# Hashed attention and channel mix on one core: bucket rows on GpSimd, joined bits in the first pair, and a new order

## The chip, the core and the metric

The kernel runs on one core of a Trainium2 chip. The metric is the device time of one execution in microseconds (us); the time of a kernel is the median of its runs. A profile is one execution, taken by the hardware profiler. TensorE multiplies matrices (PE in the profile, PEld its weight loads), VectorE (DVE) and GpSimd (POOL) do elementwise work, ScalarE (ACT) does functions such as the exponential, and SyncE (SP) issues transfers (DMAs). Each engine takes its instructions in the order in which the program gives them.

## What is computed

Attention in which a query sees only keys of its own hash bucket (six sign bits of a projection), for 4 batches of 8 heads, 768 positions, 64 channels; then a channel mix over the 512 channels of each batch.

```python
q_bits = (np.einsum('bhsd,dk->bhsk', q, proj) > 0)
k_bits = (np.einsum('bhsd,dk->bhsk', k, proj) > 0)
mask = q_bucket[:, :, :, None] == k_bucket[:, :, None, :]
scores = np.where(mask, scale * np.matmul(q, k.transpose(0, 1, 3, 2)), -1e9)
attn = softmax(scores); x = heads joined(np.matmul(attn, v))
xk = mu_k * x + (1.0 - mu_k) * x_prev      # x_prev: x one position earlier
xr = mu_r * x + (1.0 - mu_r) * x_prev
kk = np.maximum(xk @ w_k, 0.0)
out = sigmoid(xr @ w_r) * (kk * kk @ w_v)
```

## The kernel before

The work goes by pairs of heads, 16 of them, four to a batch. For a pair, q and k of its two heads are loaded (`nat`), scaled and split into a high and a low half-precision part (`nh`: `hi`, line 495 or 555; `lo`, line 498 or 560), and transposed into `a`, 128 rows deep with positions along the free axis: from pair 2 on by one transposing DMA (line 502), for pairs 0 and 1 by TensorE (line 573) with a copy out of PSUM (lines 578 and 580).

The bucket mask is part of the score matmul: six rows of `a`, 64 to 69, hold the sign bits of q (scaled) and of k, so that equal buckets add a constant that the exponential's bias takes off again. To get these rows, TensorE multiplies `a` by the projection (`bits`, line 521), VectorE turns the signs into numbers in `bx` (line 524), 32 partitions to each of the four blocks q0, q1, k0, k1, and four DMAs on SyncE's queue move six partitions each from `bx` to rows 64 to 69 of `a` (`row`, line 534). For pair 0 alone each block has its own matmul (line 597) and its own sign operation, which writes the rows of `a` at once (line 605 on VectorE, 603 on ScalarE); `DIRECT = (0,)` says so.

Scores come in nine steps of 1024 columns a pair (`sc`, line 637), each followed by one exponential on ScalarE into `pt` (line 641). Then the product with v (`oo`, line 666), the normalization (lines 677 to 684), a transpose of the result, by TensorE (`ot`, line 694) or by DMA (`otd`, line 700), the mix with the previous position (`df`, `xk`, `xr`, lines 725 to 740). GpSimd sums v (lines 446 to 458) and casts the weights (line 405). Once the four pairs of a batch are there, the channel mix runs: `kp` (line 758) with a relu (762) and a square (765), `r` (779) with a tanh (782), `v` (789), the last product (796) and the store (799) for each of six chunks of 128 positions.

Every operation is recorded by `add` with the engine it runs on, and issued in the order of the list `ORDER`, a permutation of all operations written out in the file. So the order on each engine is that of `ORDER`, and a waiting operation holds all that stand behind it on its engine. PSUM has eight banks; `schedule` gives a bank, or a pair of them, to each result that asks for one with `take`, as a plan with estimated durations finds them free.

Of the kernel before, what the change touches and what calls it, by code (L numbers as in the profile page):

```python
# [12 lines left out]
U16 = mybir.dt.uint16  # L13
# [4 lines left out]
LAG = {"PE": 0.21, "ACT": 0.21, "DVE": 0.15, "POOL": 0.18, "SP": 1.8, "GQ": 2.0}  # L18

PR = {  # L20
    'ldq': -2.811, 'ldv': -2.337, 'hi': -5.393, 'lo': -1.084, 'tr': -2.122, 'bits': -1.224, 'bx': -4.393, 'row': 4.034,
    'va': 0.273, 'vsum': -2.003, 'mean': -0.515, 'pv0': 0.767, 'pv1': 1.128, 'fin': -1.916, 'ot': 1.215, 'xt': -1.326,
    'df': -1.607, 'xk': -3.487, 'xr': 2.133, 'moe': 4.97, 'mk': 2.095, 'mv': 2.279, 'sq': 0.189, 'os': 0.275,
    'tpe': -4.352, 'tev': -0.289, 'va_u': 2.059, 'vsum_u': -3.477,
    'otd': 1.3, 'wk': 1.5, 'wkd': 0.2, 'wr': 3.0, 'wrd': 0.1, 'wv': 3.4, 'wvd': 0.1, 'wc': 0.5, 'p0b': -8.0, 'p0j': 0.6, 'p0n': 8.0,
}


PX = {}


def X(kind, n):
    return PX.get(f"{kind}@{n}", 0.0)


def R(kind, n):
    return n + PR[kind] + X(kind, n)


ORDER = [  # L40
    16, 17, 23, 21, 14, 20, 55, 56, 19, 25, 0, 2, 3, 4, 63, 64, 83, 5, 84, 6, 7, 8, 10, 69,
    58, 89, 70, 13, 57, 73, 65, 66, 26, 27, 85, 28, 29, 30, 67, 90, 91, 92, 86, 87, 68, 74, 75, 76,
    79, 80, 93, 94, 61, 71, 106, 114, 107, 108, 60, 115, 22, 18, 102, 31, 81, 88, 82, 110, 109, 77, 95, 165,
    159, 116, 11, 96, 12, 59, 136, 137, 72, 132, 133, 103, 104, 111, 112, 166, 105, 15, 212, 158, 211, 113, 62, 134,
    167, 138, 78, 117, 135, 168, 118, 119, 264, 121, 139, 126, 127, 123, 169, 170, 218, 130, 131, 120, 122, 219, 140, 98,
    99, 100, 101, 147, 124, 148, 220, 221, 222, 223, 128, 141, 149, 150, 125, 142, 35, 129, 143, 191, 192, 151, 193, 144,
    145, 146, 194, 189, 271, 190, 171, 172, 177, 181, 178, 182, 174, 179, 180, 161, 187, 188, 272, 152, 153, 154, 185, 186,
    162, 32, 163, 164, 195, 183, 184, 155, 156, 224, 225, 176, 246, 247, 200, 242, 243, 240, 241, 201, 265, 424, 425, 244,
    97, 245, 196, 197, 198, 175, 173, 232, 233, 202, 214, 215, 234, 235, 199, 230, 231, 238, 273, 36, 203, 239, 204, 205,
    206, 207, 229, 274, 275, 208, 33, 34, 210, 227, 292, 160, 296, 157, 216, 217, 253, 293, 290, 226, 209, 248, 236, 228,  # L50
    297, 288, 291, 254, 294, 249, 267, 268, 269, 237, 289, 426, 255, 256, 286, 250, 251, 295, 284, 252, 257, 213, 287, 427,
    280, 285, 270, 417, 303, 282, 414, 415, 428, 281, 277, 479, 480, 283, 278, 418, 276, 435, 419, 436, 279, 449, 450, 304,
    305, 298, 445, 306, 299, 300, 446, 307, 301, 37, 441, 442, 443, 444, 420, 302, 41, 308, 421, 38, 422, 423, 42, 39,
    447, 432, 437, 448, 438, 309, 430, 258, 504, 505, 456, 500, 501, 259, 310, 260, 261, 43, 457, 458, 429, 433, 434, 311,
    502, 503, 481, 262, 459, 40, 322, 482, 312, 323, 431, 324, 492, 493, 460, 266, 472, 473, 474, 470, 314, 439, 440, 315,
    469, 483, 580, 498, 499, 488, 489, 416, 527, 528, 451, 525, 325, 452, 453, 330, 316, 496, 534, 535, 475, 454, 455, 331,
    497, 477, 263, 494, 495, 338, 339, 461, 326, 487, 327, 328, 476, 485, 555, 556, 559, 560, 511, 340, 512, 513, 490, 491,
    478, 317, 334, 557, 558, 342, 343, 524, 589, 332, 329, 344, 590, 335, 536, 537, 538, 484, 486, 333, 547, 548, 529, 506,
    346, 345, 347, 348, 543, 544, 507, 508, 341, 553, 554, 362, 45, 551, 552, 313, 509, 510, 318, 514, 515, 471, 582, 44,
    583, 319, 320, 591, 545, 546, 584, 350, 351, 349, 321, 336, 592, 593, 363, 364, 358, 585, 359, 360, 586, 587, 541, 539,  # L60
    600, 601, 588, 354, 355, 356, 530, 549, 550, 46, 384, 531, 526, 721, 602, 603, 722, 723, 47, 48, 532, 533, 566, 385,
    724, 725, 726, 727, 542, 540, 614, 615, 567, 568, 462, 337, 352, 569, 579, 728, 729, 598, 599, 570, 561, 378, 374, 379,
    610, 718, 353, 611, 375, 773, 612, 613, 562, 596, 616, 563, 606, 607, 357, 617, 595, 604, 605, 564, 565, 370, 371, 372,
# [39 lines left out]
class Plan:  # L103
    def __init__(self, pairs, banks, most, moe_most):
        self.ops = []
        self.writer = {}
        self.readers = {}
        self.pairs, self.banks, self.most, self.moe_most = pairs, banks, most, moe_most
        self.slot = {}

    def add(self, eng, dur, prio, fn, r=(), w=(), take=None, give=(), lag=None, name="", at=0.0, svc=0.0, off=None, tr=0, port=0, land=1.1):
        o = Op()
        o.i = len(self.ops)
        dur = round(dur, 5)
# [741 lines left out]
```

## Time and profile before

| | |
|---|---|
| Three runs | 255.88, 257.94, 258.53 us; median 257.94 |
| Profiled execution | span 258.4 us; its own time is not listed apart from the three |
| Busy | TensorE 234.6, VectorE 183.9, ScalarE 183.5, GpSimd 54.8 us |
| Exponentials (line 641) | 144, 139.7 us in all |
| Score matmuls (line 637) | 384, first at 12.2, last at 199.2 us |
| Bucket row DMAs (line 534) | 60 of 9.0 KB, first issued at 18.4, last at 184.5 us |
| Granted TensorE clock | mean 0.993 |

A line of the profile names an engine, a line of the kernel, an operation, and what it writes and reads (`a<-bx`: from `bx` into `a`, buffer numbers left out), then times. "X <- Y" in a list of waits says that X stood idle until Y was done. The "chain" is the work that ended last, followed back from the end to what released each step. A busy TensorE is not TensorE at its peak, since matmuls are pipelined. A "q" behind an engine's name is its queue of issues, where DMAs are started.

### The profile page before, as it was taken

The numbers are of one execution on the slowest core, as the hardware profiler recorded it, in microseconds if no ns is written. First come the engines' busy times: TensorE is split into PE (matmuls) and PEld (weight loads), VectorE is DVE, ScalarE is ACT, GpSimd is POOL, SyncE is SP. The second block draws the span as 40 slices with busy tenths as digits, with TensorE's granted clock in tenths as the row PEclk, the third lists the DMA queues.
The fourth block names the chain that finished last, engine by engine and source line by source line (L and its number), as shares of the span: only waits on it lengthen the run. The fifth ranks groups of instructions, "written<-read, shape, count | busy, mean of one in ns | idle before, by whom it ended". The sixth has DMA issues, their size and how long they took to land.

```text
span 258.4 us, 6132 instructions
## 1 busy us (share of the span) xinstructions
PE 234.6 (91%) x2435; PEld 140.1 (54%) x2453; DVE 183.9 (71%) x391; ACT 183.5 (71%) x242; POOL 54.8 (21%) x89
## 2 busy tenths in 40 slices
PE   8898888695988798999996999999999999999994
PEld 3445466463655375555564556764576554555441
DVE  4999868588497584999996597665869785355322
ACT  3498989888788798778867699998797364245321
POOL 5064045622242524007003020026000000000000
PEclk9999999999999999999998899999999999999999
DMA  6997997898999699969999666485515111212033
GB/s 192 283 308 163 193 239 158 250 309 156 322 183 267 188 315 269 215 165 287 158 250 267 125 154 173 140 200 92 146 35 114 41 41 39 87 41 84 0 123 121
DMA packets 72957, 44.54 MB, mean 172 GB/s; under 512 B 55160, under 2 KB 67808, under 8 KB 72928
## 3 DMA queue, kind: packets, MB, share of 16 engines
q1 hardware_dynamic: 72848, 44.15, 68.0%
q8 instruction: 19, 0.31, 0.5%
q14 instruction: 10, 0.08, 0.1%
q10 hardware_dynamic: 80, 0.00, 0.0%
HBM read 24.12 MB, written 6.29 MB: 118 GB/s over the span
## 4 chain that ended last, share of the span: by engine, by line
PE 55%; DMA 22%; DVE 10%; ACT 4%; SPq 3%; issue 3%; DVEq 0%
PE ps_all L789 14%; PE ps_all L637 12%; PE ps_all L758 11%; DMA a<-nh 8%; DMA a<-bx 7%; PE ps_all L666 7%; PE ps_all L779 7%; DMA nat<-in_k_dram 5%; ACT pt L641 4%; PE ps_all L521 3%; DVE nh L498 2%; DMA nat<-in_q_dram 2%; SPq L534 1%; DVE df L725 1%; DVE nh L495 1%
## 5 line engine op out<-in xcount | busy, mean ns | idle before, releaser
L641 ACT ACTIVATE pt<-ps_all 128x1024 bf16<-128x1024 f32 x144 | 139.7, 1039 | 24.2 <-PE ps_all L637 23.4
L637 PE MATMUL ps_all<-a 128*128 128x512 f16 (+1 forms) x384 | 81.5, 328 | 8.8 <-DMA a<-bx 7.8
L637 PEld LDWEIGHTS <-a 128*128 128x128 f16 x384 | 33.3, 98 | 32.0 <-DMA a<-bx 9.1
L758 PE MATMUL ps_all<-xk,wk 128*128 128x384 bf16 x256 | 49.0, 326 | 1.0 <-DVE ob L684 1.0
L666 PEld LDWEIGHTS <-pt 128*128 128x128 bf16 x1152 | 43.6, 98 | 8.9 <-ACT pt L641 1.0
L762 ACT ACTIVATE kr<-ps_all 128x384 bf16<-128x384 f32 x64 | 30.8, 499 | 23.7 <-PE ps_all L758 16.7
L789 PE MATMUL ps_all<-wv,k 128*128 128x512 bf16 x185 | 46.3, 379 | 0.4
L666 PE MATMUL ps_all<-va,pt 128*128 128x65 bf16 x1152 | 45.6, 195 | 0.6 <-ACT pt L641 0.6
L758 PEld LDWEIGHTS <-wk 128*128 128x128 bf16 x256 | 24.5, 98 | 19.2 <-issue 2.2
L452 POOL TENSOR_TENSOR vt<-vn 128x384 f32<-128x384 f32 x12 | 12.8, 1064 | 79.6 <-DMA vn<-in_v_dram 79.5
L789 PEld LDWEIGHTS <-k 128*128 128x128 bf16 x192 | 18.5, 98 | 20.4 <-issue 0.3
L796 DVE SCALAR_TENSOR_TENSOR os<-rs,ps_all 128x512 f32<-128x512 f32 x24 | 16.3, 684 | 18.3 <-PE ps_all L789 16.3
L765 DVE TENSOR_TENSOR k<-kr 128x384 bf16<-128x384 bf16 x64 | 21.3, 357 | 11.2 <-ACT kr L762 11.0
L498 DVE SCALAR_TENSOR_TENSOR nh<-nat,nh 128x1536 f16<-128x1536 f32 (+1 forms) x16 | 26.8, 1677 | 0.3
L782 ACT ACTIVATE rs<-ps_all 128x512 f32<-128x512 f32 x24 | 14.3, 602 | 16.3 <-PE ps_all L779 10.0
L779 PE MATMUL ps_all<-wr,xr 128*128 128x512 bf16 x85 | 23.2, 379 | 0.5
L524 DVE TENSOR_SCALAR bx<-ps_all 128x768 uint16<-128x768 uint16 x15 | 14.4, 957 | 12.2 <-ACT kr L762 4.2
L495 DVE TENSOR_SCALAR nh<-nat 128x1536 f16<-128x1536 f32 (+1 forms) x16 | 14.7, 916 | 8.2 <-DMA nat<-in_k_dram 6.2
L521 PE MATMUL ps_all<-a,p 128*32 128x256 f16 (+1 forms) x240 | 13.7, 328 | 5.4 <-DMA a<-nh 5.0
L684 DVE TENSOR_TENSOR ob<-ps_all,rc 128x384 bf16<-128x384 f32 x32 | 17.7, 555 | 0.7
L477 DVE SCALAR_TENSOR_TENSOR va<-ps_all,vn 128x384 bf16<-128x384 f32 x24 | 12.5, 550 | 5.0 <-PE ps_all L472 5.0
L779 PEld LDWEIGHTS <-xr 128*128 128x128 bf16 x96 | 9.1, 98 | 9.3
(71 smaller groups left out, 161.9 us busy)
## 6 DMA issues: line engine op xcount, KB each, us to landing
vn<-in_v_dram SPq DMA_DIRECT2D x16, 384.0 KB
out_dram<-os SPq DMA_DIRECT2D x24, 256.0 KB
nat<-in_k_dram SPq DMA_DIRECT2D x15, 384.0 KB
nat<-in_q_dram SPq DMA_DIRECT2D x15, 384.0 KB
wst<-in_moe_w_k_dram SPq DMA_DIRECT2D x2, 512.0 KB
wst<-in_moe_w_r_dram SPq DMA_DIRECT2D x2, 512.0 KB
wst<-in_moe_w_v_dram SPq DMA_DIRECT2D x2, 512.0 KB
a<-bx SPq DMA_DIRECT2D x60, 9.0 KB
```

Of the source, the lines that this page charges most:

```text
L495: nc.vector.tensor_scalar(out=nh[:, :, 0:D], in0=nat.rearrange("p j (c d) -> p (j c) d", d=D), scalar1=QS, scalar2=None, op0=ALU.mult)
L498: nc.vector.scalar_tensor_tensor(out=nh[:, :, D:P], in0=nat.rearrange("p j (c d) -> p (j c) d", d=D), scalar=QS, in1=nh[:, :, 0:D], op0=AL ...
L521: nc.tensor.matmul(ps[32 * i : 32 * i + 32, lo:hi], w_, a_t[sa][:, i, lo:hi], start=st, stop=not st)
L637: nc.tensor.matmul(ps[:, lo - s * STEP : hi - s * STEP], side_a["k"][sa][:, j, jc * P : (jc + 1) * P], side_a["q"][sa][:, j, q0 : q0 + hi ...
L641: nc.scalar.activation(out=pt_t[sp][:, s * STEP : (s + 1) * STEP], in_=ps_t[plan.slot[nm]], func=AF.Exp, bias=EBIAS, scale=ESC)
L666: nc.tensor.matmul(oo[:, ic * 65 : ic * 65 + 65], pt_t[sp][:, o : o + P], va_t[sa][:, j, jc, 0 : D + 1], start=(not uc and ic == 0 and jc ...
L684: nc.vector.tensor_tensor(out=ob_t[so][:, :, j * D : (j + 1) * D], in0=oo[:, :, 0:D], in1=rc_t[sr][:, 1, :].unsqueeze(2).to_broadcast([P, ...
L758: nc.tensor.matmul(ps[:, 0:HALF], wk_sb[:, d, fc * P : (fc + 1) * P], xk_t[mx[d]][:, h * HALF : (h + 1) * HALF], start=(d == 0), stop=(d = ...
L762: nc.scalar.activation(out=kr_t[sk], in_=sm(nm)[:, 0:HALF], func=AF.Relu, scale=0.5 ** 0.5)
L765: nc.vector.tensor_tensor(out=k2_t[s2][:, h * HALF : (h + 1) * HALF], in0=kr_t[sk], in1=kr_t[sk], op=ALU.mult)
L779: nc.tensor.matmul(sm(nr), xr_t[mx[d]][:, c * P : (c + 1) * P], wr_sb[:, d, :], start=(d == 0), stop=(d == NDC - 1))
L789: nc.tensor.matmul(sm(nv), k2_t[(b * NFC + fc) % NK2][:, c * P : (c + 1) * P], wv_sb[:, fc, :], start=(fc == 0), stop=(fc == NFC - 1))
```

## The change

- The rows 64 to 69 of `a` are written by GpSimd copies from `bx` (as 32-bit words, two numbers each), where they were by DMAs.
- In pair 0, head 0 keeps its direct bits; head 1 of q and k go through one joined `bits` matmul, one sign operation over 64 partitions, and two GpSimd copies.
- The scaling `hi` of head 1 of q in pair 0, and all four of pair 1, move from VectorE to GpSimd.
- The load of k's head 0 of the first pair is issued from ScalarE's queue, behind that of the projection.
- The last chunk of the last batch (chunk 5 of batch 3) has its second product, its last operation and its store in two halves of 256 columns.
- `ORDER` is new throughout, and the PSUM banks are a written-out list `BANKS`, no longer found by a plan. The code of the planner goes, which issues nothing.

```diff
+BANKS = [
+    7, 6, 6, 7, 7, 7, 7, 5, 6, 5, 4, 0, 7, 6, 7, 5, 2, 0, 2, 2, 0, 1, 0, 1, 1, 0, 7, 6, 7, 0, 1, 0, 2, 2, 1, 1, 1, 2, 0, 7, 6, 7, 2, 0, 2,
...
     def schedule(self):
...
+        self.slot = dict(zip(self.names, BANKS))
+        return [self.ops[i] for i in ORDER]
...
-    FIRST = {(n, side, j): ("DVE", "DVE", "DVE") for n in range(2) for side in "qk" for j in range(2)}
-    FIRST[(0, "k", 0)] = ("ACT", "ACT", "ACT")
-    FIRST[(0, "k", 1)] = ("ACT", "ACT", "ACT")
-    V_GQ = ()
+    FIRST = {
+        (0, "q", 0): ("DVE", "DVE", "DVE"), (0, "k", 0): ("ACT", "ACT", "ACT"),
+        (0, "q", 1): ("POOL", "DVE", None), (0, "k", 1): ("ACT", "ACT", None),
+        (1, "q", 0): ("POOL", "DVE", None), (1, "k", 0): ("POOL", "DVE", None),
+        (1, "q", 1): ("POOL", "DVE", None), (1, "k", 1): ("POOL", "DVE", None),
+    }
...
-                    def f(side=side, j=j):
-                        nc.sync.dma_start(out=side_nat[side][s][:, j, :],
+                    lq = "ACT" if side == "k" and j == 0 else "SP"
+
+                    def f(side=side, j=j, lq=lq):
+                        (nc.scalar if lq == "ACT" else nc.sync).dma_start(out=side_nat[side][s][:, j, :],
...
-    def add_bits(n):
+    def add_bits(n, blocks):
         sa, sx = n % NAQ, n % NBX
         nm = f"bits{n}"
+        rows = 32 * len(blocks)
...
-                    for i in range(4):
-                        nc.tensor.matmul(ps[32 * i : 32 * i + 32, lo:hi], w_, a_t[sa][:, i, lo:hi], start=st, stop=not st)
+                    for i, (side, j) in enumerate(blocks):
+                        nc.tensor.matmul(ps[32 * i : 32 * i + 32, lo:hi], w_, side_a[side][sa][:, j, lo:hi], start=st, stop=not st)
...
-        for i in range(4):
-            def row(i=i):
-                (nc.scalar if n in ROW_ACT and i % 2 else nc.sync).dma_start(out=a_t[sa][D : D + NB, i, :], in_=bx_t[sx][32 * i : 32 * i + NB, :])
...
+        for i, (side, j) in enumerate(blocks):
+            def row(i=i, side=side, j=j):
+                nc.gpsimd.tensor_copy(side_a[side][sa][D : D + NB, j, :].bitcast(FP32), bx_t[sx][32 * i : 32 * i + NB, :].bitcast(FP32))
+            add("POOL", 0.55, row, r=[("bx", sx)], w=[("ab", side, sa, j, h) for h in range(2)], port=1, name=f"row{n}{side}{j}")
...
-                    if e_hi == "DVE":
-                        nc.vector.tensor_scalar(out=o, in0=nv, scalar1=QS, scalar2=None, op0=ALU.mult)
+                    if e_hi != "ACT":
+                        (nc.vector if e_hi == "DVE" else nc.gpsimd).tensor_scalar(out=o, in0=nv, scalar1=QS, scalar2=None, op0=ALU.mult)
...
-                    if n not in DIRECT:
+                    if not halves:
                         continue
...
-        if n not in DIRECT:
-            add_bits(n)
+        add_bits(n, [("q", 1), ("k", 1)] if n == 0 else [("q", 0), ("q", 1), ("k", 0), ("k", 1)])
...
+            cuts = ((0, 256), (256, 512)) if b == B - 1 and c == NSC - 1 else ((0, 512),)
+            for x0, x1 in cuts:
+                nv = f"v{b}_{c}_{x0}"
...
+                            nc.tensor.matmul(sm(nv)[:, x0:x1], k2_t[(b * NFC + fc) % NK2][:, c * P : (c + 1) * P], wv_sb[:, fc, x0:x1],
...
+                    nc.vector.scalar_tensor_tensor(out=os_t[so][:, x0:x1], in0=rs_t[s1][:, x0:x1], scalar=1.0, in1=sm(nv)[:, x0:x1], op0=ALU.add, op1=ALU.mult)
...
+                    nc.sync.dma_start(out=out[b].rearrange("(p c) m -> c p m", c=NSC)[c][:, x0:x1], in_=os_t[so][:, x0:x1])
```

## The prediction, made before the change was run

> **What bounds the kernel now.** I read the chain of waits first, then the busy time by stage, then who waits for whom, then the timeline at the longest of those waits. The listed times run from 255.88 to 258.53 us, median 257.94. The profiled execution has a span of 258.4 and no time of its own on the page; the highest listed time lies 0.1 above that span, so I set 0.1 around it. The sum is made against 258.4 and carried to the median, 0.5 lower. A difference within 1% (2.6 us) can't be told from none: the three times alone lie that far apart.
>
> The chain of waits, shares of the span by engine, then by line:
>
> ```profile
> PE 55%; DMA 22%; DVE 10%; ACT 4%; SPq 3%; issue 3%; DVEq 0%
> PE ps_all L789 14%; PE ps_all L637 12%; PE ps_all L758 11%; DMA a<-nh 8%; DMA a<-bx 7%; PE ps_all L666 7%; PE ps_all L779 7%; DMA nat<-in_k_dram 5%; ACT pt L641 4%; PE ps_all L521 3%; DVE nh L498 2%; DMA nat<-in_q_dram 2%; SPq L534 1%; DVE df L725 1%; DVE nh L495 1%
> ```
>
> Over half is TensorE, but 22% is transfers: transposes (`a<-nh`), bucket rows (`a<-bx`), loads. Rows alone are 7%, some 17 us; that isn't yet what their removal is worth, because TensorE has other work beside most of it. The stages (cut at the first score, two late row waits, the last exponential and the last matmul) show where TensorE is idle; per engine busy us and count, then clock, DMA share, GB/s:
>
> ```profile
> 0.00:12.25 12.25, 10.00 (x60) 4.89 (x61) 8.78 (x20) 5.27 (x8) 3.53 (x25) 1.00 0.78 236
> 12.25:62.30 50.05, 42.05 (x578) 26.81 (x576) 41.21 (x66) 42.95 (x47) 21.26 (x23) 1.00 0.98 226
> 62.30:103.00 40.70, 34.40 (x413) 21.82 (x415) 27.05 (x56) 33.68 (x45) 14.68 (x18) 1.00 0.94 251
> 103.00:200.30 97.30, 94.10 (x1097) 58.84 (x1104) 77.87 (x182) 80.01 (x99) 15.29 (x24) 0.98 0.73 169
> 200.30:254.70 54.40, 54.09 (x301) 27.76 (x303) 28.33 (x69) 21.59 (x45) 0.00 (x0) 1.00 0.17 64
> ```
>
> From 103 on TensorE is busy nearly all the time (3.2 idle, then 0.3): there only less work, or fewer of the last waits, would help. Its idle time lies in 12 to 103: 8.0 and 6.3 us. ScalarE, which does the exponentials, is idle there for 7.1 and 7.0, and the DMA engines are 98% and 94% busy. So neither engine is the bound of these stages; they wait for data. For which (us, times, longest):
>
> ```profile
> ACT pt L641 <- PE ps_all L637: 23.4, 30, 1.7
> ...
> PE ps_all L637 <- DMA a<-bx: 7.8, 6, 2.2
> ...
> PE ps_all L521 <- DMA a<-nh: 5.0, 5, 1.9
> ```
>
> Rows hold TensorE for 7.8 us in 6 waits (its weight loads see the same waits), transposes for 5.0 in 5. By the same view cut by stage, the rows' share is 4.8 in 12 to 62, 1.0 in 62 to 103, 2.1 after; the transposes' is 0.3, 4.1, 0.6. The longest row wait, in order of time (start, length):
>
> ```profile
> 41.03 0.96 DVE L524 TENSOR_SCALAR bx<-ps_all 128x768 uint16<-128x768 uint16 x1
> 41.30 3.84 SPq L502 DMA_TRANSPOSE a<-nh  x1
> ...
> 46.90 2.96 SPq L534 DMA_DIRECT2D a<-bx  x4
> ...
> 51.85 1.02 PE L637 MATMUL ps_all<-a 128*128 128x512 f16 x5 [2.20 <-DMA a<-bx]
> ...
> 52.48 1.94 ACT L641 ACTIVATE pt<-ps_all 128x1024 bf16<-128x1024 f32 x2 [1.68 <-PE ps_all L637]
> ```
>
> The bucket bits of pair 4 were ready at 42.0. Their four row copies stand on SyncE's queue behind a transpose that takes 3.84 us to issue and behind loads, are issued from 46.90, and the last lands at 51.7: nearly 10 us from bits to use, of which TensorE lost 2.2 and ScalarE 1.7.
>
> **The change, part by part.** *Rows on GpSimd.* 60 DMAs leave SyncE's queue; 62 copies of 6 x 384 float words are added on GpSimd. No such copy is in the trace. GpSimd's casts give it a size: fixed cost by the smallest, slope by the 1024-wide one (min/median/max ns):
>
> ```profile
> L365 POOL CAST p<-npj x2: 208/334/460, 3.8 to 4.3; 64x6 f16<-64x6 f32 x2
> L405 POOL CAST wk<-wst x2: 1036/1036/1036, 38.8 to 54.1; 128x1024 bf16<-128x1024 f32 x2
> ```
>
> (1036 - 208) / 1018 = 0.81 ns an element, so 208 + 378 x 0.81 = 0.51 us each, between 0.21 and 1.04; an estimate. Four take 2.1 us against the 3.3 us that a row DMA takes from issue to landing at 48.44 on the chain, and against 9.7 us with the queue. GpSimd goes from 54.8 busy to about 90 us, most of it before 185: no bound. But it works in order, so a row behind a sum over v (line 452) waits for that v load, and GpSimd waits 79.5 us in all for such loads now. I counted exponentials in both order lists. Before, the last row of a pair comes 1 to 5 exponentials behind that pair's first score, in all of pairs 2 to 15; after, it comes 1 to 7 (about 1 us each) ahead in ten of them, level in pairs 9, 13 and 14, and two behind only in pair 10, where the late row is of the head scored last. The v loads that stand ahead of rows 3, 4 and 6 on GpSimd are issued some five exponentials earlier; casts of weights that stand ahead of rows 5 and 6 only two. So I take 4.5 of the 4.8 us, all of 1.0, and 2.0 of 2.1 as saved: -7.5 (bounds 0, if each wait only gets another name, and -7.9).
>
> *SyncE's queue without rows.* Loads and transposes are no longer behind them: 60 issues at a median of 0.70 us, 42 us of queue time. The transposes that hold TensorE for 4.1 us in 62 to 103 move ahead in the new order: the one of pair 6 stands at exponential 33, not 47. But the DMA engines are 94% busy there, so a transpose issued earlier still shares them. I take half, -2.0 (0 to -4.1).
>
> *The start.* The first score is at 12.25, held by a transpose of pair 1 that waited 0.93 us for a DVE copy (line 578). From DVE's queue ahead of that point go five scale operations of 0.35 us (q head 1 of pair 0, all four of pair 1; on GpSimd 0.51 each, beside DVE) and the 0.95 us bit operation of q head 1. In its place `bx0` (0.95) and two copies (1.0) stand ahead of the second score. Adding the new DVE order up from the 3.26 at which q lands, with its rows' durations, head 1's scale on GpSimd at 4.65 and k's first part at 5.87: last operation before the first score at 10.2, score at 10.7, first exponential 11.3 instead of 12.88; second one, behind `bx0` at 11.1 and two copies, 12.9 instead of 13.85. From there the 0.5 us that ScalarE spends on k bits between exponentials (14.84) is gone too. I take -1.3 (+0.5, if the copies are held by DVE, to -2.0). The k load on ScalarE's queue is put at 0: ScalarE takes head 1 of k first in both versions, and that load stays third on SyncE; the table load (1.28, ending 2.59) hides its issue, with k landing at 5.31. The Trainium skill (DMA: Bandwidth & Descriptors, Issuing engines are not separate DMA queues) says that queues of several engines share the same 16 DMA engines and that only issue time is saved; by it this part would be the 0.4 us of one issue at most, and no run here shows a second queue with a large load.
>
> *Last chunk in halves.* Same matmul columns. The last DVE operation is 0.69 for 512; half of that, less its fixed part, gives 0.40. -0.3 (0.3 to -0.6, a further store being issued).
>
> *Order and banks.* The second layer's matmuls of batch 2 now start at exponential 119, not 142. This moves TensorE work from after 200 into a stage where it idles 3.2 us of 97: nothing to win by itself. Set at 0 (plus or minus 3, what is idle there).
>
> *GpSimd beside DVE.* Some DVE operations grow when GpSimd runs beside them, others not:
>
> ```profile
> L498 DVE SCALAR_TENSOR_TENSOR nh<-nat,nh x16: 948/1756/2477, 13.9 to 167.8; 128x1536 f16<-128x1536 f32 x12, 128x768 f16<-128x768 f32 x4
> L725 DVE TENSOR_TENSOR df<-xt x16: 517/558/1390, 29.5 to 212.0; 128x768 bf16<-128x768 bf16 x16
> L524 DVE TENSOR_SCALAR bx<-ps_all x15: 951/958/958, 17.3 to 178.9; 128x768 uint16<-128x768 uint16 x15
> ```
>
> At 35.91 a 1.76 us subtraction (498) took 2.26 with a GpSimd cast and sum beside it; at 59.41 a 0.56 us one (725) took 1.39; bits out of PSUM (524) never grew. Growth 0.5 to 0.8; I take 0.55. I count lines 495, 498, 725, 731, 737, 740 and 765, which work in SBUF alone, as those that may grow: 106 of DVE's 184 us, so 62 x 0.58 x 0.55 = 20 us more DVE work, into 42 us of its idle time (12 to 200). DVE has 10% of the chain: +2.0 (0 to +17). The Trainium skill (GPSIMD Engine Reference, Key points) says that GpSimd shares its SBUF interfaces with VectorE and contends with operations in a 2-port mode or with two SBUF inputs. The trace agrees: 498 and 725, which grew, have two such inputs; 524 reads PSUM. By the rule every copy that meets such an operation pays, which is the last rival below.
>
> Sum: -7.5 - 2.0 - 1.3 - 0.3 + 2.0 = -9.1. 258.4 - 9.1 = 249.3; by the median 248.8.
>
> **Rivals.** *DMA-bound:* the rows go, but with the DMA engines 98% busy the next late thing is the load or transpose behind. For: 60 row DMAs are 0.5 of 44 MB; DVE already waits 6.2 us for k loads. Against: only 0.3 us of TensorE's waits in 12 to 62 are for transposes. Row gains halve (-3.7), the queue's gain goes, rest as before: -3.7 - 1.3 - 0.3 + 2.0 = -3.3, 254.6. *All cover closes:* ScalarE runs without a gap from 12 to 103. It could win 14.1; with -1.3, -2.0 and -0.3 that is -17.7; I take -14 (243.9), since ScalarE must at times wait for TensorE. *DVE becomes the bound, slower:* every copy meets an operation that can grow: 62 x 0.55 = 34 us, DVE 180 of 188 us busy in 12 to 200, and the copies themselves are held (a 413 ns sum, line 455, took up to 1804 ns). It decides once growth exceeds some 0.35 us a copy, 90% busy, TensorE's own share now. Half of 34 on the path: -9.1 - 2.0 + 17 = +5.9, 263.8. For: the stretches above; a copy always comes right after DVE's own bits, when DVE takes up its next operation. Against: 42% of DVE's work can't grow, and copies are now spread.
>
> **How the numbers follow.** Forecast 0.50, DMA-bound 0.20, all cover closes 0.16, DVE bound 0.14. Predicted 249, its own range 245.5 to 252.5. From 244 to 259 lie the forecast, the DMA-bound case and half of the better one: 0.78, and the near edge of the slower one. Faster by over 1% (under 255.4): 0.50 + 0.16 + 0.08 of the DMA-bound case, 0.74; its other 0.12 is the same; slower 0.14.
>
> **What would show it.** Right: waits on rows gone from TensorE's list, or under 1 us on GpSimd copies; a copy at about 0.5 us; first exponential near 11.3; TensorE idle in 12 to 103 down from 14 to about 6; DVE busy up by up to 20. Wrong: transposes or loads wait in the rows' place, lines 495, 498 or 725 of the old numbering near their maxima throughout, or TensorE's idle time after 103 grown by the new order.

## The result, and the profile after

The changed kernel takes 259.2 us (median of 19 runs, 256.68 to 259.61), the kernel before 257.65 us (19 runs, 255.45 to 262.99). The ratio is 1.0059, with a 95% interval of 1.003 to 1.0088: a little slower, and within the 1% that the prediction calls no change. 249.0 was predicted, 244 to 259. Ratios here are formed against undisturbed runs of the kernel before on the same chip, so they need not equal the quotient of two medians.

The profiled execution has a span of 257.5 us. It looks 0.9 shorter than the one before (258.4) while the medians say 1.5 longer. The runs explain this: they list time and span together, 259.24 us with 257.5, so 1.74 us lies around a span and not the 0.1 that the prediction set. The profiled execution of before was then one of some 260.1 us (an estimate from that difference), well above its median; the one of after lies at its median. So the old trace is some 2.5 us longer than a median execution (260.1 less 257.65), where in it isn't known, and a comparison of the two traces' totals carries that doubt.

The chain of waits of the changed kernel, shares of the span by engine, then by line (scores are now line 527, rows 434, the bit operation 424, bits 421, exponentials 531):

```profile
PE 60%; POOL 17%; DVE 7%; issue 5%; DMA 5%; ACT 4%; SPq 0%; POOLq 0%; DVEq 0%; ACTq 0%
PE ps_all L527 15%; PE ps_all L675 14%; PE ps_all L642 13%; PE ps_all L554 7%; PE ps_all L662 7%; POOL a L434 6%; ACT pt L531 3%; POOL vt L352 3%; PE ps_all L421 3%; DMA a<-nh 3%; POOL wk L304 3%; DMA nat<-in_k_dram 2%; POOL nh L450 2%; DVE k L649 1%; DVE nh L397 1%
```

DMA fell from 22% to 5%; GpSimd (POOL), which was not in the old chain, now has 17%. Only 6% of the span are the row copies themselves. The rest is what they have to queue with: sums of v (`vt`, 352), casts of weights (`wk`, 304), scaling (`nh`, 450). The waits of the changed kernel in total (us, times, longest):

```profile
POOL a L434 <- DVE bx L424: 71.2, 10, 15.7
ACT pt L531 <- PE ps_all L527: 25.3, 23, 4.1
...
PE ps_all L527 <- POOL a L434: 7.5, 4, 3.4
...
PE ps_all L549 <- POOL xt L260: 2.1, 1, 2.1
...
PE ps_all L642 <- POOL wk L304: 1.7, 2, 0.9
```

TensorE's 7.8 us for row DMAs became 7.5 us for row copies, in 4 waits, not 6. Two new waits stand beside them: the constant term of the product with v (549), 2.1 us, and the first layer of the mix (642), 1.7 us. (The profile names a memset, line 260, as the releaser of the first; it stands right behind the sum over v that the matmul reads.) The first line is GpSimd waiting for bits, 71.2 us: waits at the head of a queue, which hold all that stands behind them. Most of them cost nothing, since 70.7 us are left in the run below that puts the queue in order. By stage, at the cuts of before, the last one at the last matmul (busy us and count per engine, then clock, DMA share, GB/s):

```profile
0.00:12.25 12.25, 9.79 (x54) 4.57 (x55) 7.39 (x15) 4.73 (x8) 8.50 (x23) 1.00 0.84 270
12.25:62.30 50.05, 41.10 (x534) 26.28 (x533) 38.06 (x57) 38.61 (x42) 37.85 (x52) 0.90 0.91 226
62.30:103.00 40.70, 37.17 (x448) 23.64 (x448) 37.05 (x67) 33.94 (x47) 29.72 (x33) 1.00 0.84 221
103.00:200.30 97.30, 94.90 (x1005) 57.11 (x1015) 78.05 (x167) 77.55 (x102) 34.59 (x49) 1.00 0.73 169
200.30:254.00 53.70, 53.38 (x409) 30.20 (x412) 31.68 (x84) 27.28 (x45) 0.50 (x1) 1.00 0.19 66
```

The stage of 62 to 103 went as hoped: TensorE's idle time fell from 6.3 to 3.5. The one of 12 to 62 went wrong: TensorE idles 9.0 us (8.0 before), ScalarE 11.4 (7.1 before), GpSimd is busy for 37.9 of 50, and the clock granted to TensorE is 0.90 where it was 1.00. Two stretches of the timeline show where (start, length; "xN" are N operations joined in one line):

```profile
12.86 1.02 ACT L531 ACTIVATE pt<-ps_all 128x1024 bf16<-128x1024 f32 x1 [0.99 <-PE ps_all L527]
...
13.29 2.63 POOL L434 COPY a<-bx 6x384 f32<-6x384 f32 x2
...
15.97 1.26 PE L527 MATMUL ps_all<-a 128*128 128x512 f16 x6 [2.38 <-POOL a L434]
...
16.40 4.88 ACT L531 ACTIVATE pt<-ps_all 128x1024 bf16<-128x1024 f32 x5 [2.51 <-PE ps_all L527]
...
27.92 0.94 DVE L424 TENSOR_SCALAR bx<-ps_all 128x768 uint16<-128x768 uint16 x1
28.06 0.85 POOL L352 TENSOR_TENSOR vt<-va 128x390 f32<-128x390 bf16 x1
28.99 0.42 POOL L355 TENSOR_TENSOR vt<-vt 128x130 f32<-128x130 f32 x1
29.49 1.01 POOL L358 TENSOR_TENSOR vsu<-vt 128x130 bf16<-128x130 f32 x1
30.47 1.75 DVE L397 SCALAR_TENSOR_TENSOR nh<-nat,nh 128x1536 f16<-128x1536 f32 x1
...
30.58 2.35 POOL L352 TENSOR_TENSOR vt<-va 128x390 f32<-128x390 bf16 x1
33.01 0.61 POOL L355 TENSOR_TENSOR vt<-vt 128x130 f32<-128x130 f32 x1
33.68 2.79 POOL L434 COPY a<-bx 6x384 f32<-6x384 f32 x4
```

The bits of pair 2 are there at 28.9. Their rows come after two sums over v in GpSimd's queue, the second with a first part of 2.35 us beside a VectorE subtraction (30.47), where the same operation took 0.85 at 28.06. The rows start at 33.68, 4.8 us after their data; TensorE starts the scores at 35.41 after a wait of 3.37. At the start, the second exponential comes at 16.40 (13.85 before), behind two copies that take 2.63 us together.

### The profile page after: what moved, and what is told of

Same layout as the page of the kernel before. It is cut to its first block, busy times and chain, and to the rows that moved or that the text cites. A ratio compares the mean times of both kernels' runs of the same rounds, so it can differ in the third digit from the quotient of the medians.

```text
span 257.5 us, 6113 instructions
## 1 busy us (share of the span) xinstructions
PE 236.3 (92%) x2443; PEld 141.8 (55%) x2461; DVE 192.6 (75%) x387; ACT 182.1 (71%) x241; POOL 111.2 (43%) x156
## 4 chain that ended last, share of the span: by engine, by line
PE 60%; POOL 17%; DVE 7%; issue 5%; DMA 5%; ACT 4%; SPq 0%; POOLq 0%; DVEq 0%; ACTq 0%
PE ps_all L527 15%; PE ps_all L675 14%; PE ps_all L642 13%; PE ps_all L554 7%; PE ps_all L662 7%; POOL a L434 6%; ACT pt L531 3%; POOL vt L352 3%; PE ps_all L421 3%; DMA a<-nh 3%; POOL wk L304 3%; DMA nat<-in_k_dram 2%; POOL nh L450 2%; DVE k L649 1%; DVE nh L397 1%
## 5 line engine op out<-in xcount | busy, mean ns | idle before, releaser
L527 PE MATMUL ps_all<-a 128*128 128x256 f16 (+1 forms) x384 | 84.0, 332 | 8.9 <-POOL a L434 7.5
L434 POOL COPY a<-bx 6x384 f32<-6x384 f32 x62 | 43.8, 706 | 76.5 <-DVE bx L424 71.2
L554 PEld LDWEIGHTS <-pt 128*128 128x128 bf16 x1152 | 44.9, 98 | 14.0 <-issue 3.8
L527 PEld LDWEIGHTS <-a 128*128 128x128 f16 x384 | 34.0, 99 | 33.6 <-POOL a L434 8.6
L554 PE MATMUL ps_all<-va,pt 128*128 128x65 bf16 x1152 | 47.3, 194 | 0.0
L675 PE MATMUL ps_all<-wv,k 128*128 128x512 bf16 (+1 forms) x193 | 46.1, 370 | 0.5
L649 DVE TENSOR_TENSOR k<-kr 128x384 bf16<-128x384 bf16 x64 | 25.0, 415 | 12.4 <-ACT kr L646 12.4
L642 PEld LDWEIGHTS <-wk 128*128 128x128 bf16 x256 | 23.8, 98 | 18.4 <-POOL wk L304 2.5
L682 DVE SCALAR_TENSOR_TENSOR os<-rs,ps_all 128x512 f32<-128x512 f32 (+1 forms) x25 | 16.5, 663 | 16.8 <-PE ps_all L675 7.7
L397 DVE SCALAR_TENSOR_TENSOR nh<-nat,nh 128x1536 f16<-128x1536 f32 (+1 forms) x16 | 26.9, 1685 | 0.2
L424 DVE TENSOR_SCALAR bx<-ps_all 128x768 uint16<-128x768 uint16 (+1 forms) x16 | 15.2, 952 | 7.6 <-PE ps_all L421 7.0
L394 DVE TENSOR_SCALAR nh<-nat 128x1536 f16<-128x1536 f32 (+1 forms) x16 | 17.0, 1070 | 0.0
L421 PE MATMUL ps_all<-a,p 128*32 128x512 f16 (+1 forms) x248 | 14.4, 347 | 0.2 <-DMA a<-nh 0.2
```

The costliest lines, as they stand in the source:

```text
L397: nc.vector.scalar_tensor_tensor(out=nh[:, :, D:P], in0=nat.rearrange("p j (c d) -> p (j c) d", d=D), scalar=QS, in1=nh[:, :, 0:D], op0=AL ...
L421: nc.tensor.matmul(ps[32 * i : 32 * i + 32, lo:hi], w_, side_a[side][sa][:, j, lo:hi], start=st, stop=not st)
L434: nc.gpsimd.tensor_copy(side_a[side][sa][D : D + NB, j, :].bitcast(FP32), bx_t[sx][32 * i : 32 * i + NB, :].bitcast(FP32))
L527: nc.tensor.matmul(ps[:, lo - s * STEP : hi - s * STEP], side_a["k"][sa][:, j, jc * P : (jc + 1) * P], side_a["q"][sa][:, j, q0 : q0 + hi ...
L554: nc.tensor.matmul(oo[:, ic * 65 : ic * 65 + 65], pt_t[sp][:, o : o + P], va_t[sa][:, j, jc, 0 : D + 1], start=(not uc and ic == 0 and jc ...
L642: nc.tensor.matmul(ps[:, 0:HALF], wk_sb[:, d, fc * P : (fc + 1) * P], xk_t[mx[d]][:, h * HALF : (h + 1) * HALF], start=(d == 0), stop=(d = ...
```

## The experiments

Three theories stood at first. *Queue:* rows on GpSimd gain nothing because GpSimd takes its work in order, and rows, sums, casts and scaling stand in an order that makes TensorE wait for the wrong one. *VectorE:* copies and VectorE's operations hold each other, and that pays back the gain. *Order:* the new order is the worse one and hides what the rows are worth.

**The scaling off GpSimd.** The five `hi` operations of the start go back to VectorE.

```diff
-        (0, "q", 1): ("POOL", "DVE", None), (0, "k", 1): ("ACT", "ACT", None),
-        (1, "q", 0): ("POOL", "DVE", None), (1, "k", 0): ("POOL", "DVE", None),
-        (1, "q", 1): ("POOL", "DVE", None), (1, "k", 1): ("POOL", "DVE", None),
+        (0, "q", 1): ("DVE", "DVE", None), (0, "k", 1): ("ACT", "ACT", None),
+        (1, "q", 0): ("DVE", "DVE", None), (1, "k", 0): ("DVE", "DVE", None),
+        (1, "q", 1): ("DVE", "DVE", None), (1, "k", 1): ("DVE", "DVE", None),
```

> The changed kernel (259.2 us), but the five scale operations of the first two pairs are back on VectorE. Queue theory (GpSimd takes its work in order, and its queue took the place of SyncE's): five operations of 1.17 us leave the queue ahead of the first two row copies; the copies start right behind the bits of pair 0 (about 12.5, not 13.29), TensorE's wait of 2.38 us before 16 falls under 1, the second exponential comes at about 14.3 instead of 16.4, and the time falls by 2 to 3 us, to about 256.5. VectorE theory (GpSimd's copies hold VectorE up, the queue is no matter): VectorE gets 5 x 0.36 more ahead of the first score, which comes 1 us later; time 259 to 260.5. Order theory (the new order is the worse one): no change, 259.

Measured: 258.08 us (257.64 to 259.89), ratio 1.0046 [1.0011, 1.0082]. The wait of 2.38 before the second score is gone, but the first exponential moves to 15.62, because VectorE, in the same order, now waits 1.92 us at such an operation (7.81) for a load of k. A wait taken from one in-order queue went into another. The time is none of the three that were expected (256.5, 259 to 260.5, 259).

**The new order with rows by DMA.**

```diff
-                nc.gpsimd.tensor_copy(side_a[side][sa][D : D + NB, j, :].bitcast(FP32), bx_t[sx][32 * i : 32 * i + NB, :].bitcast(FP32))
-            add("POOL", 0.55, row, r=[("bx", sx)], w=[("ab", side, sa, j, h) for h in range(2)], port=1, name=f"row{n}{side}{j}")
+                nc.sync.dma_start(out=side_a[side][sa][D : D + NB, j, :], in_=bx_t[sx][32 * i : 32 * i + NB, :])
+            add("SP", 0.55, row, r=[("bx", sx)], w=[("ab", side, sa, j, h) for h in range(2)], port=1, name=f"row{n}{side}{j}")
```

> The changed kernel with its new order, but all rows (62) go by DMAs on SyncE's queue again. Queue theory: waits on GpSimd copies (7.5 us on TensorE) go, GpSimd falls by some 44 us, and waits on row DMAs of about the same size come back; transposes wait longer again; 258 to 262. VectorE theory: VectorE loses the 9 us by which it had grown, time falls to about 256. Order theory: as the rows themselves are worth something and the order costs more, it gets worse, 262 to 266.

Measured: 282.63 us (282.09 to 283.65), ratio 1.1003 [1.0933, 1.1073]. TensorE waits 12.3 us in 8 for row DMAs and 10.5 us in 4 for transposes, the longest of 6.1, which stand behind rows that wait for bits on SyncE. All theories expected less (256 to 266). The order is made for rows elsewhere and can't be judged apart from them.

**The old order with rows on GpSimd.** In the kernel before, only the row's own line changes.

```diff
-                (nc.scalar if n in ROW_ACT and i % 2 else nc.sync).dma_start(out=a_t[sa][D : D + NB, i, :], in_=bx_t[sx][32 * i : 32 * i + NB, :])
+                nc.gpsimd.tensor_copy(a_t[sa][D : D + NB, i, :].bitcast(FP32), bx_t[sx][32 * i : 32 * i + NB, :].bitcast(FP32))
```

> The kernel before (257.65 us) with its old order and all else old; only the 60 row DMAs are GpSimd copies, at the same place in the list. Queue theory: GpSimd here has no scale operations, but its sums over v wait for loads, and rows stand behind them; half of the 7.8 us of row waits goes and transposes come earlier: 252 to 255. Order theory: without the new order the rows are worth what was predicted, 7 us and more: 248 to 250. VectorE theory: VectorE grows by about 9 us, and nothing is won: 257 to 260.

Measured: 263.77 us (263.22 to 264.18), ratio 1.0263 [1.0199, 1.0326]. The timeline of this kernel (rows are line 534 there, sums 446 to 458):

```profile
18.39 3.81 POOL L534 COPY a<-bx 6x384 f32<-6x384 f32 x4 [12.05 <-DVE bx L524]
...
22.27 1.42 POOL L446 CAST va<-vn 128x768 bf16<-128x768 f32 x1
23.78 0.85 POOL L452 TENSOR_TENSOR vt<-va 128x390 f32<-128x390 bf16 x1
24.70 0.41 POOL L455 TENSOR_TENSOR vt<-vt 128x130 f32<-128x130 f32 x1
25.20 0.41 POOL L458 TENSOR_TENSOR vsu<-vt 128x130 bf16<-128x130 f32 x1
...
25.66 0.48 PE L661 MATMUL ps_all<-vsu,tiny 128*128 128x390 bf16 x1 [6.77 <-POOL vsu L458]
```

GpSimd does nothing for 12 us until the bits of pair 1 come, with the sum of pair 0 behind them; TensorE then waits 6.77 us for that sum, and 3.65 later for the next. The work behind a waiting copy is the larger trouble: TensorE waits 10.4 us in all for these sums, and 2.5 for copies. No theory expected more than 260 us, and the order theory, 248 to 250, falls with it.

**The old order, two places of GpSimd's queue moved.** Only the list `ORDER` of the last kernel changes: the cast and the sums of pair 0 (98 to 101) go ahead of the rows of pair 1 (from 121 on), and, not shown, the first row of pair 2 (174) behind the sums of pair 1.

```diff
-    167, 138, 78, 117, 135, 168, 118, 119, 264, 121, 139, 126, 127, 123, 169, 170, 218, 130, 131, 120, 122, 219, 140, 98,
-    99, 100, 101, 147, 124, 148, 220, 221, 222, 223, 128, 141, 149, 150, 125, 142, 35, 129, 143, 191, 192, 151, 193, 144,
+    138, 78, 117, 135, 168, 118, 119, 264, 98, 99, 100, 101, 121, 139, 126, 127, 123, 169, 170, 218, 130, 131, 120, 122, 219, 140, 147, 124,
```

> The old order with rows on GpSimd (263.8 us), with two places of GpSimd's order changed: the cast and sums of v of pair 0 ahead of the rows of pair 1, and the first row of pair 2 behind the sums of pair 1. Queue theory: TensorE's waits of 6.8 and 3.7 us on those sums go; 254 to 257. Order theory or VectorE theory: under 2 us of change, 262 to 264.

Measured: 255.85 us (254.76 to 257.0), ratio 0.9995 [0.9953, 1.0037], against 263.77 for the last kernel. The waits of 6.77 and 3.65 are gone; the longest on a row copy left is 3.44. This is what the queue theory expected (254 to 257; the others 262 to 264). With the same engine, the same copies and sums, the same order on every other engine and the same PSUM banks, some 7 to 8 us hung on two places in one queue (7.9 by the medians, 2.7% by the ratios, whose intervals don't meet). But with that put right, rows on GpSimd are only level with rows by DMA in the old order.

**Rows on VectorE.**

```diff
-                nc.gpsimd.tensor_copy(side_a[side][sa][D : D + NB, j, :].bitcast(FP32), bx_t[sx][32 * i : 32 * i + NB, :].bitcast(FP32))
-            add("POOL", 0.55, row, r=[("bx", sx)], w=[("ab", side, sa, j, h) for h in range(2)], port=1, name=f"row{n}{side}{j}")
+                nc.vector.tensor_copy(side_a[side][sa][D : D + NB, j, :].bitcast(FP32), bx_t[sx][32 * i : 32 * i + NB, :].bitcast(FP32))
+            add("DVE", 0.55, row, r=[("bx", sx)], w=[("ab", side, sa, j, h) for h in range(2)], port=1, name=f"row{n}{side}{j}")
```

> The changed kernel with its new order, but the 62 row copies run on VectorE, not on GpSimd, at the same place in the list. A copy there should take about 0.27 us (384 words at two a cycle and a fixed part), 17 us in all. Queue theory: GpSimd falls to about 67 us busy, TensorE's waits on rows go from 7.5 to under 3 us, and the time falls to 253 to 256. VectorE theory: GpSimd's share of the strain goes but VectorE gets 17 us of its own: no change, 258 to 260. Order theory: no change, 259.

Measured: 267.33 us (266.38 to 268.0), ratio 1.0412 [1.0335, 1.0488]. Copies are shorter (median 352 ns, 512 on GpSimd), GpSimd is busy for only 65.3 us, but VectorE for 210.7, and TensorE now waits for VectorE at many places (`ob` 3.3 us, `bx` 3.1, `a` 3.0). No theory expected more than 260 us. In this order, which was made for rows on GpSimd, GpSimd is the better of the two.

**Longer copies.** The same bytes as 768 half-precision elements, where the change has 384 words.

```diff
-                nc.gpsimd.tensor_copy(side_a[side][sa][D : D + NB, j, :].bitcast(FP32), bx_t[sx][32 * i : 32 * i + NB, :].bitcast(FP32))
+                nc.gpsimd.tensor_copy(side_a[side][sa][D : D + NB, j, :], bx_t[sx][32 * i : 32 * i + NB, :])
```

> The changed kernel (259.2 us) with each row copy as 768 half-precision elements, not 384 words: the same bytes, about 0.82 us a copy instead of 0.51, 19 us more on GpSimd. Queue theory: GpSimd's queue is on the path where rows and sums are late (some 20 operations), so 4 to 8 us are lost, 263 to 267. VectorE theory: a longer copy meets more VectorE operations, and VectorE grows by another 5 to 10 us; time 262 to 266, told apart from the queue by VectorE's busy time. If GpSimd was no bound: 259.

Measured: 270.69 us (268.76 to 272.43), ratio 1.061 [1.0467, 1.0753]. The operation view of this kernel (min/median/max ns):

```profile
L434 POOL COPY a<-bx x62: 816/832/2235, 14.0 to 210.7; 6x768 f16<-6x768 f16 x62
```

Each copy costs 0.32 us more by the median, 20 us in all (GpSimd 131.2 busy, 111.2 in the changed kernel); VectorE grows by 9.5 us beside it (202.1 for 192.6), 0.47 us for each us added. The time rises by 11.5 us, as much as over half of what is added to GpSimd's queue, and more than either theory expected (263 to 267, 262 to 266). It fits both, a longer queue and a slower VectorE; this run doesn't tell them apart.

**GpSimd's queue put in order.** From the kernel with the scaling on VectorE, ten operations change places in `ORDER`, at four spots (the first two are shown): part of the sum of pair 2 (215, 216) goes behind the rows of that pair; the cast and sums of pair 3 (267 to 270) ahead of the rows of pair 4; three casts of weights (36, 40, 42) ahead of the rows of pair 6; one sum of pair 9 (776) behind the last row of its pair.

```diff
-    167, 187, 141, 193, 149, 129, 170, 218, 221, 222, 219, 188, 191, 162, 163, 164, 215, 143, 194, 144, 189, 171, 150, 34, 145, 192, 151,
-    146, 183, 190, 32, 172, 152, 185, 184, 179, 216, 174, 176, 175, 186, 211, 173, 180, 181, 200, 223, 177, 201, 220, 182, 178, 153, 242,
+    167, 187, 141, 193, 149, 129, 170, 218, 221, 222, 219, 188, 191, 162, 163, 164, 143, 194, 144, 189, 171, 150, 34, 145, 192, 151, 146,
+    183, 190, 32, 172, 152, 185, 184, 179, 174, 176, 175, 186, 211, 173, 215, 216, 180, 181, 200, 223, 177, 201, 220, 182, 178, 153, 242,
...
-    246, 424, 425, 197, 234, 414, 198, 202, 235, 240, 160, 203, 286, 199, 204, 205, 206, 241, 247, 287, 274, 236, 248, 275, 237, 292, 277,
-    426, 20, 278, 267, 293, 279, 268, 269, 270, 22, 12, 280, 249, 281, 253, 294, 276, 23, 295, 250, 288, 213, 289, 290, 254, 255, 291, 284,
+    246, 424, 425, 197, 234, 414, 198, 202, 235, 240, 160, 203, 286, 199, 204, 205, 206, 241, 247, 287, 274, 236, 248, 275, 237, 292, 267,
+    268, 269, 270, 277, 426, 20, 278, 293, 279, 22, 12, 280, 249, 281, 253, 294, 276, 23, 295, 250, 288, 213, 289, 290, 254, 255, 291, 284,
```

> The kernel with the scale operations back on VectorE (258.1 us), and only GpSimd's own order changed at four places: the four rows of pair 2 ahead of the sum over v of pair 2, the cast and sum of v of pair 3 ahead of the rows of pair 4, three weight casts ahead of the rows of pair 6 (GpSimd stood idle for 3.3 us there), the sum of pair 9 behind its rows. Queue theory: those four places hold the waits of 3.4, 2.1, 1.7 and 1.35 us that TensorE has on GpSimd; about 6 of the 8.5 us go, and the half-speed clock behind the longest; time 252 to 254. VectorE theory: what counts is that the two engines hold each other up, not who comes first; waits only move; 257 to 259.

Measured: 251.52 us (250.57 to 252.16), ratio 0.9857 [0.9779, 0.9936]: 6.6 us less than the 258.08 that it starts from (1.9%, some 5 us, by the ratios, whose intervals don't meet). The waits of this kernel, and the rows of pair 2 in its timeline:

```profile
ACT pt L531 <- PE ps_all L527: 16.2, 21, 4.1
...
PE ps_all L527 <- POOL a L434: 3.6, 5, 1.4
```

```profile
30.15 4.53 POOL L434 COPY a<-bx 6x384 f32<-6x384 f32 x4
...
33.00 0.61 PE L527 MATMUL ps_all<-a 128*128 128x512 f16 x3 [1.38 <-POOL a L434]
```

Against the kernel that it starts from, the rows start 3.3 us earlier (33.46 there), although the four now take 4.53 us (2.79 there) beside VectorE; TensorE's wait there falls from 3.37 to 1.38, all its waits on copies from 5.2 to 3.6, the one of 2.1 on a sum (549) to 0.5; the 1.7 on casts (642) gives way to 1.4 on VectorE. The stage from 12 to 62 by engine, first in the kernel that it starts from, then in this one:

```profile
12.25:62.30 50.05, 42.91 (x569) 27.73 (x566) 41.34 (x62) 40.60 (x46) 36.47 (x50) 0.93 0.97 247
```

```profile
12.25:62.30 50.05, 44.25 (x620) 28.76 (x617) 45.50 (x68) 44.89 (x50) 42.03 (x54) 1.00 1.10 264
```

GpSimd is busier than before the edit (42.0 for 36.5), and so are all the others: what GpSimd lost was time at waits in the wrong order. The clock is 1.00 there again. Over the whole span VectorE is as busy as before the edit (193.7 for 193.5 us), and the order on every engine but GpSimd is the same, so the gain is the queue's and not VectorE's. The queue theory expected 252 to 254, the VectorE theory 257 to 259.

**The k load on SyncE.** From the kernel with the scaling on VectorE.

```diff
-                    lq = "ACT" if side == "k" and j == 0 else "SP"
+                    lq = "SP"
```

> The kernel with the scale operations on VectorE (258.1 us), and the load of k's head 0 back on SyncE's queue, behind that of head 1, as before the change. In the changed kernel ScalarE got its first k data at 6.16 us, before the change at 5.31. If the second queue made the two k loads share the transfer engines and so made head 1 late, ScalarE starts at about 5.3 again and the first exponential comes 0.5 to 0.8 us earlier: 257.3. If the later landing has another reason (loads of pair 1 issued 0.5 us earlier), it stays at 6.1 and nothing changes: 258.

Measured: 258.23 us (257.5 to 259.35), ratio 1.0127 [1.0042, 1.0213]; without the edit 258.08. ScalarE has k's first data at 5.04, not 6.55; the first exponential comes at 13.83, not 15.62. This first data is head 1's, whose load stays on SyncE's queue in both: it lands earlier when head 0's load isn't issued from a second queue ahead of it. Not all of the 1.8 us need be the load's: TensorE's granted clock from 10 to 15 us is 0.50 without the edit and 1.00 with it. The total doesn't move: 1.3 us are left where TensorE's wait for the rows of pair 2 ends (33.87 for 35.19), and 0.3 at its wait behind the sum of pair 3 (54.06 for 54.38).

**The start put in order.** On top of the queue put in order: the k load on SyncE, and each of the five scale operations right before the subtraction that uses it (`ORDER` again; the diff shows the load, and of the order the place of the first of them, 83).

```diff
-                    lq = "ACT" if side == "k" and j == 0 else "SP"
+                    lq = "SP"
...
-    55, 0, 56, 25, 2, 3, 4, 5, 6, 7, 8, 58, 14, 57, 11, 13, 10, 21, 17, 61, 83, 60, 26, 27, 95, 28, 29, 30, 63, 64, 69, 65, 84, 87, 85, 70,
+    55, 0, 56, 25, 2, 3, 4, 5, 6, 7, 8, 58, 14, 57, 11, 13, 10, 21, 17, 61, 60, 26, 27, 95, 28, 29, 30, 63, 64, 69, 65, 83, 84, 87, 85, 70,
```

> The kernel with GpSimd's order changed at four places (251.5 us), with k's head 0 loaded by SyncE's queue again, and the five scale operations of the first two pairs, on VectorE, each moved to stand right ahead of its subtraction; so far they stood where GpSimd had them, and VectorE waited there for loads of pair 1. The first exponential was at about 15.6 with the scale operations on VectorE. Queue theory, now for VectorE's queue: it comes at 12 to 13, and 1 to 2.5 us are won, 249 to 250.5. If the start is hidden by what follows (the load of k moved the first exponential by 1.8 us and the time not at all), 251 to 252.

Measured: 250.77 us (249.14 to 251.79), ratio 0.9751 [0.9701, 0.9801]. The first two exponentials begin at 13.18 and 14.59 (14.96 and 17.00 without the edit), but the time lies between the two that were expected (249 to 250.5, 251 to 252), and the runs overlap with those of the kernel that it starts from (250.57 to 252.16): a gain isn't shown.

**Direct bits for head 1.** On top of the last one, head 1 of pair 0 has its own bits and direct rows again, as in the kernel before.

```diff
-        (0, "q", 1): ("DVE", "DVE", None), (0, "k", 1): ("ACT", "ACT", None),
+        (0, "q", 1): ("DVE", "DVE", "DVE"), (0, "k", 1): ("ACT", "ACT", "ACT"),
...
-        add_bits(n, [("q", 1), ("k", 1)] if n == 0 else [("q", 0), ("q", 1), ("k", 0), ("k", 1)])
+        if n:
+            add_bits(n, [("q", 0), ("q", 1), ("k", 0), ("k", 1)])
```

> As the run beside it (start rearranged), but head 1 of pair 0 has its own bits again, q's by VectorE (0.95 us), k's by ScalarE (0.8 us), no joined matmul and no two row copies. The second score then waits for VectorE's operation and not for that and two copies of 0.5 to 1.3 us behind it: the second exponential 1 to 2 us earlier, ScalarE 0.8 us more. If the joined bits cost at the start: 0.5 to 1 us faster than the run beside it. If the start is hidden by what follows: the same within 0.5 us.

Measured: 249.24 us (248.87 to 250.68), ratio 0.9714 [0.9674, 0.9754], the fastest kernel here. The first exponential is at 11.96, the second, expected 1 to 2 us earlier, comes 0.6 later, at 15.21. The time is 1.5 us below the last kernel, but the two intervals overlap: that the joined bits cost anything isn't settled. That this kernel lies at the 249 predicted for the change is luck: it differs from the change by five edits, and the sum of the prediction isn't confirmed by it.

## Why the prediction was wrong

**The step that failed** is "Rows on GpSimd", -7.5. In its words: "each wait only gets another name" was its lower bound, at 0, and that is what happened: 7.8 us of TensorE's waits on row DMAs became 7.5 on row copies, and 2.1, 1.7 and 0.6 us of waits on sums and casts in the same queue came new. It reasoned that GpSimd at 90 us busy is "no bound", an average over the span, and it judged earliness by counting exponentials between a pair's rows and its first score in the list. It named the danger ("a row behind a sum over v (line 452) waits for that v load") and looked at when the loads and casts ahead of rows 3 to 6 are issued, but it added up neither the work that stands ahead of each row on GpSimd nor what is held behind it, and took 4.5 of 4.8 as saved. In the order list the last row of pair 2 stands three exponentials, some 3 us, ahead of that pair's first score; in the trace the sums ahead of these rows keep GpSimd busy from 28.06 to 33.6, with no wait for a load, and TensorE waits 3.37. Two pairs of runs show the queue's order as the cause: two places moved in the old order, 263.77 to 255.85; four moved in the new one, 258.08 to 251.52, with rows, copies, their engine and the order on all other engines the same. Even with the queue in order TensorE waits 3.6 us on copies and 0.5 on a sum, about half of the 7.8 that the rows cost before. TensorE's idle time from 12 to 103, forecast to fall from 14 to about 6, is 12.5 (9.0 and 3.5) in the changed kernel. The rival *all cover closes* is out with it: ScalarE's idle time from 12 to 62 rose from 7.1 to 11.4.

Measured against the kernel before, 257.65: rows on GpSimd cost 6 us in the old order, and are level there with two places of the queue put right. The new order is worth 4.6 us to rows on GpSimd (263.77 to 259.2, the small parts of the change included), and costs 25 with rows by DMA. The change as given is the sum of a loss and a gain of nearly the same size.

**The size of a copy** held, and yet its sum didn't. The operation view of the changed kernel (min/median/max ns):

```profile
L434 POOL COPY a<-bx x62: 496/512/1915, 13.3 to 200.4; 6x384 f32<-6x384 f32 x62
```

```profile
L450 POOL TENSOR_SCALAR nh<-nat x5: 1167/1168/1540, 3.7 to 11.5; 128x384 f16<-128x384 f32 x5
```

0.51 us was predicted, 512 ns is the median. But 62 x 0.512 = 31.7, and the copies took 43.8: 12 us were added to some of them, up to 1915 ns for one. The scale operation, sized from the same casts, was off by more than two: 1.17, not 0.51. GpSimd came to 111.2 us, not 90.

**SyncE's queue** (-2.0, 0 to -4.1) was right and too small: TensorE's waits on transposes at the bits fell from 5.0 to 0.2 us. With rows on GpSimd they are small in the old order too (0.5 us, and 1.9 with two places moved), so most of it comes from the rows leaving the queue and not from the new order. The rival in which the DMA engines hold back the next transfer is refuted by the same numbers.

**The start** (-1.3) fell. The first exponential stayed (12.86 for 12.88), the second came 2.55 us later. The scaling on GpSimd, at 1.17 to 1.54 each, ends late (VectorE waits 1.06 us at 5.19 for the first); the two copies took 2.63, not 1.0. "The k load on ScalarE's queue is put at 0" was wrong for the landing: ScalarE takes head 1 first, as the prediction says, and has its data at 6.16, not 5.31 (with the scaling on VectorE at 6.55, and at 5.04 with head 0's load back on SyncE). It held for the total, which was 258.08 with the load on ScalarE's queue and 258.23 without. The Trainium skill (DMA: Bandwidth & Descriptors, Issuing engines are not separate DMA queues) says that transfers from several engines' queues interleave on the same 16 DMA engines, and that a second queue saves issue time only. The runs agree that there is nothing to win, and the interleaving fits the landing: with head 0's load issued from the second queue, the data of head 1, needed first, came 1.5 us later (6.55 for 5.04).

**GpSimd beside DVE** (+2.0, of 20 us more busy time): VectorE went from 183.9 to 192.6, 8.7 more, or 10.5 with the 1.8 us of scaling (5 x 0.36) that left it. That is half the growth predicted. Of the lines counted as those that may grow, the subtraction (498, now 397), on which the size of the growth was read, doesn't grow in all (26.9 us for 26.8); the squares (765, now 649) go from 21.3 to 25.0 and the scaling (495, now 394) from 14.7 to 17.0. The rival in which VectorE becomes the bound did not come about, with 75% busy. What the growth costs isn't shown: in the longer copies it comes together with a longer queue, and the queue put in order gains its time with VectorE's busy time unchanged.

**The last chunk** (-0.3): from the end of the last group of matmuls to the end of the span it is 3.5 us (254.0 to 257.5), 3.7 before, so -0.2.

**Order and banks** (0, plus or minus 3): that wasn't a term of its own, as the runs show; the order and the engine of the rows have one price together. (The prediction's "second layer's matmuls of batch 2" are those of the first layer, `kp`.)

Added up from the two profiles, with the doubt said above: TensorE's visible idle time fell from 23.8 (258.4 - 234.6) to 21.2 us (257.5 - 236.3), 2.6 less, where the prediction had some 9; the transposes give 4.8 of it, and rows and their new neighbours take back 4.1 (7.5 + 2.1 + 1.7 + 0.6 - 7.8), and the other 1.9 lies in waits too small to tell apart. And TensorE's busy time grew by 1.7 us, which no step had. The granted clock may be the reason (mean 0.977, before 0.993), but that isn't shown: with the scaling on VectorE it is 0.977 too, and TensorE is busy for 234.4 us, no more than before.

## What to carry to other kernels

Work that moves from a DMA queue to an in-order engine is priced by walking that engine's queue: for each moved operation, what stands ahead of it, when that can run, and what is held behind it while it waits; the engine's mean load says nothing of it. An order written out by hand belongs to the engines it was made for, so it is judged with them, and after such a move the few longest waits "on the new engine" name the places to swap: changes at four places of one queue were worth 5 to 7 us here, more than the change itself moved. A busy time per operation is given with its median and its maximum where two engines hold each other.

## What the hardware showed that was not expected

TensorE's granted clock can fall after waits of only 2 to 3.4 us, so that a wait can cost more than its length. The changed kernel around its waits of 2.38 (until 15.97) and 3.37 us (until 35.41), columns as in the stages above, the clock the third number from the end:

```profile
16.00:20.00 4.00, 4.00 (x24) 2.57 (x24) 1.49 (x4) 3.60 (x4) 3.07 (x7) 0.64 0.91 135
...
35.40:39.00 3.60, 3.59 (x23) 1.23 (x24) 0.97 (x2) 1.11 (x2) 1.00 (x2) 0.50 0.97 176
39.00:43.00 4.00, 4.00 (x50) 2.96 (x49) 2.87 (x3) 3.24 (x4) 3.75 (x4) 0.75 0.44 163
```

The kernel before after its wait of 2.20 us (until 51.85), and after one of 2.06 (until 140.2):

```profile
52.00:56.00 4.00, 4.00 (x74) 3.08 (x73) 3.10 (x6) 3.13 (x4) 1.04 (x1) 1.00 0.89 305
...
140.20:144.00 3.80, 3.79 (x44) 2.90 (x44) 3.77 (x5) 1.02 (x1) 0.93 (x1) 0.55 0.60 157
```

So 2.2 us may cost nothing and 2.06 may halve the clock for some 4 us; in the changed kernel a wait of 2.09 (until 55.54) isn't followed by a fall either, the clock is 1.00 from there to 59.5. In the old order with rows on GpSimd it is 0.50 for 4.4 us after the wait of 6.77. In the changed kernel the two places account for about (4.0 x 0.36 + 3.6 x 0.50 + 4.0 x 0.25) = 4.2 us of lost clock, an upper estimate of their price, since a busy TensorE isn't bound by its clock alone. With the queue in order the mean clock is 0.997 and TensorE is busy for 233.7 us; the kernel that this starts from, at 0.977, has 234.4, so the measured difference is only 0.7. The Trainium skill (TensorE: Matmul & The Clock Gate, What's actually happening) puts the fall to half the clock after at least one idle window of about 3.4 us, a window that runs freely. That the clock fell after waits of 2.06 and 2.38 us differs from it, since no whole window fits into them, and here the measurement decides; why it didn't after 2.09 and 2.20, no run here shows.
